# Steps of the triangular inverses moved from VectorE to GpSimd, with new durations for the planner of the order

## The chip, the cores and the metric

One core of one Trainium2 chip runs the kernel. The metric is the device time of one execution in microseconds (us): 1148.85 us before the change, the median of 3 runs. The engines are named as in the profile: PE (TensorE), DVE (VectorE), ACT (ScalarE), POOL (GpSimd), SP (SyncE, which here issues all DMAs).

## The reference

A recurrent attention over 768 time steps (4 batches x 8 heads, head size 40) is followed by two dense layers over its 3072 x 320 output.

```python
for t in range(S):                       # S = 768
    y[:, :, t] = einsum('bhd,bhde->bhe', r[t], state)
    Sa = einsum('bhde,bhe->bhd', state, a[t])
    state = state * w[t][:, :, None, :] - einsum('bhd,bhe->bhde', Sa, b[t]) + einsum('bhd,bhe->bhde', v[t], k[t])
x = y.transpose(0, 2, 1, 3).reshape(3072, 320)
h = x @ w_in;  x = (h * tanh(softplus(h))) @ w_out      # layer 1, d_ff = 2048
h = x @ w_in2; out = (h * cos(h)) @ w_out2              # layer 2
```

## The kernel before

The recurrence is computed in chunks of C = 32 time steps. The 32 (batch, head) units are split in two parts of 16, so there are 48 chunk tasks g = 0..47: chunk c = g // 2 of part g % 2. Two consecutive g, the two parts of one chunk in time, are a pair bt; there are 24 pairs.

For every g, `pre(g)` prepares the chunk: products of the decays by two scans on VectorE (`scan` L570, `rscan` L576), the scaled operands AM (`am_f`, L584) and KB (`kb_f`, L590), two memsets of AM on GpSimd (L598), the chunk's own coefficients by TensorE (`g1`, L607) and their masked copy out of PSUM by VectorE (`gev`, L617). These coefficients form, for each unit, a 32x32 triangular system, which goes to DRAM (`ldm`, L630).

For every pair, `inverse(bt)` inverts the 32 matrices of the pair. They are loaded into one half of XM as 64 rows (two 16x16 triangular blocks of each matrix), and 14 rounds, each a multiply into XT (L679) and an add into XM (L677), eliminate them by i = 1..14, over i x (15 - i) elements in each row: 14, 26, 36, 44, 50, 54, 56 and back. These 28 instructions depend each on the one before. A memset of the diagonal (L686) ends them, the result goes to DRAM and comes back as TT (L690, L694), and `halves` joins the two blocks with two matmul tasks and a transpose and a multiply on VectorE (L721, L724). XM has two halves, so two inverses can be under way.

For every g, `chain(g)` then carries the state on: `rhs` (L787), `zmm` (L801), transposes (L833), `rvz` (L859), its masked copy `rve` on VectorE (L869), `fmm` (L885), the next state and the output on VectorE (`sev` L896, `yev` L904) and transposes of the state (L929). The copies out of PSUM between them run on ScalarE (L390). Chunks are prepared up to LA = 7 ahead, as the ring of buffers for PE, AM and FL allows.

The output of two chunks in time makes a block of 256 tokens. There are 12 blocks in `layer1` (matmuls L988 and L969, with the activation on ScalarE at L1058 and L1060 and the low half GL on VectorE, L1063), then 24 tiles in `layer2` (L1003, L1019, and GL on GpSimd, L1146). The weights are split in high and low halves by `prep` (L461 to L508, the low halves on GpSimd).

No engine's order is written by hand. `Plan.run` simulates all tasks on the five engines with the durations given at `P.add`, always takes the task that can start first, with ties broken by a rank and a priority, and emits the instructions in that order. Each engine then executes its instructions in the emitted order, with semaphores for the dependences. So a duration in `P.add` changes no instruction, only where it stands. A task with `port=True` on VectorE or GpSimd is planned so that it overlaps no other such task of either engine. AGE bounds (in planned us) how long an attention task in another matmul mode is held back behind matmuls of the layers, and `lat` is the planned delay from a task to its successors.

The parts of the code that the change touches:

Of the kernel before, what the change touches and what calls it, by code (L numbers as in the profile page):

```python
# [85 lines left out]
LEAVE, CHANGE, ENTER = 0.22, 0.12, 0.13  # L86
AGE = 4.0
WAIT = 8.0
# [163 lines left out]
def body(ctx, tc, ins, out):  # L252
# [147 lines left out]
    def act(n, psum=True, ptr=0):  # L400
        return (0.05 if psum else 0.093) + 0.000833 * n + 0.093 * ptr

# [11 lines left out]
    DIRECT = 4  # L414
    HV_D, HV_P = (0.36, 0.41), 0.5
    B_HI2 = 1.0
    am_on, GLE = lambda g, d: ("DVE", 0.33), ("DVE",)
    HIE = EITHER
# [127 lines left out]
    def fifo(name, t):  # L546
        p = prev_fifo.get(name)
        if p is not None:
            t.preds.append(p)
        prev_fifo[name] = t  # L550
        return t

    def pre(g):
# [18 lines left out]

        t_sc = fifo("scan", P.add("DVE", 0.62, scan, preds=[t_ld, S_D], acq=[("PE", k("PE"))], prio=pr, port=True))
        def rscan():
# [4 lines left out]

        t_rp = P.add("DVE", 0.85, rscan, preds=[t_sc], acq=[("RP", k("RP"))], prio=pr, port=True)  # L580

# [17 lines left out]

        t_z0 = P.add("POOL", 0.24, az_f(0), preds=[t_a1], prio=pr)  # L600
        t_z1 = P.add("POOL", 0.24, az_f(1), preds=[t_z0], prio=pr)

# [19 lines left out]
        for c2 in range(2):  # L622
            for p in range(2):
                t_gl.append(P.add("DVE", 0.22, gev(p, c2), preds=[t_g], rel=[k("G")], prio=pr))
        Gev[g] = t_gl
# [27 lines left out]
    def inverse(bt):  # L653
# [15 lines left out]
        t = P.add("SP", 1.0, ld, preds=[ldma[g0 + i] for i in range(cnt)] + [S_X], acq=[("X", ("X", bt))], lat=DMA_LAT, prio=pr)  # L669

        def step(i, add):
            w = 15 - i

            def f():
                tv, b = xu()[:, :i * w].rearrange("p (j t) -> p j t", j=i), blk()
                if add:
                    V.tensor_tensor(out=b[:, 0:i, i + 1:16], in0=b[:, 0:i, i + 1:16], in1=tv, op=ALU.add)  # L677
                else:
                    V.tensor_tensor(out=tv, in0=bc(b[:, i:i + 1, i + 1:16], (2 * n, i, w)),  # L679
                                    in1=bc(b[:, 0:i, i:i + 1], (2 * n, i, w)), op=ALU.mult)  # L680
            return f

        for i in range(1, 15):
            for add in range(2):
                t = P.add("DVE", dve(i * (15 - i)), step(i, add), preds=[t], lat=0.13, prio=pr, port=True)
        t = P.add("DVE", 0.1, lambda: V.memset(x()[:, 16:512:33], 1.0), preds=[t], prio=pr)  # L686

# [81 lines left out]
    def chain(g):  # L769
# [11 lines left out]
        def rhs():  # L781
            rp = pa(k("R"))[:, 0:160].rearrange("p (g d) -> p g d", d=D)
            for n in range(NU):
# [8 lines left out]
        mated("rhs", c, t)  # L792
        t = P.add("ACT", act(160), lambda: A.activation(rs().rearrange("p g d -> p (g d)"), pa(k("R"))[:, 0:160],
                                                        AF.Copy, scale=-1.0),
# [79 lines left out]
        for h in range(2):  # L874
            ve[h] = P.add("DVE", 0.36, rve(h), preds=[r0] + z[2 * h:2 * h + 2] + [ve[i] for i in range(h)], rel=[k("V")], prio=pr)
        yb, yc = divmod(c, 2)
# [36 lines left out]
        for h, ft in ((0, f0), (1, f1)):  # L913
            s = []
            if not last:
                s = [P.add("DVE", 0.34, sev(h, p), preds=[ft, io[nx][2]], prio=pr) for p in range(2)]
            sevs += s
            rel = [k(f"F{h}")] + ([k("PE")] if h == 1 else [])
            y_acq = [("Y", ykey)] if (yc == 0 and h == 0) else []
            yevs.append(P.add("DVE", dve(128), yev(h), preds=[ft] + s + yevs, acq=y_acq, rel=rel, prio=pr + 1))  # L920
        Sev[g] = sevs
# [418 lines left out]
```

## Time and profile before

| | before |
|---|---|
| median of 3 runs | 1148.85 us (1147.74 to 1149.64) |
| the profiled execution | 1148.73 us |
| its span, first to last instruction | 1147.0 us |
| mean granted clock of TensorE | 0.952 |
| busy: PE, DVE, ACT, POOL | 1028.0, 832.9, 542.6, 228.0 us |
| inverse steps on VectorE (L679 and L677) | 336 + 336 instructions, 68.4 + 67.3 us |

The span holds three stages: attention with what is ready of layer 1 (up to about 650 us), the rest of layer 1 (to about 845 us) and layer 2. The engines' shares differ between them, so they are read by stage. A busy TensorE isn't TensorE at its peak, since its matmuls are pipelined and may run at a lower granted clock.

### The profile page before, as it was taken

Reading aid. Unit: us, or ns where it says so; the run is one execution under the profiler, and the core shown is the slowest. Engines: PE = TensorE matmul, PEld = TensorE weight load, DVE = VectorE, ACT = ScalarE, POOL = GpSimd, SP = SyncE. Lnnn points to the kernel's source line nnn. Section 1 sums busy time; section 2 is a strip of 40 time slices with the busy share of each in tenths; the row PEclk is TensorE's granted clock in tenths of the full one; section 3 lists DMA queues with packets and bytes.
Section 4 is the critical chain, followed back from the end, with each engine's and each line's share of the span. In section 5 each row is a group of like instructions: output and inputs, shape, how many; then the busy total and the mean of one; then the engine's idle time right before and its main releaser. Section 6 shows DMA issues by size and latency. Waiting matters only on the chain.

```text
span 1147.0 us, 36376 instructions
## 1 busy us (share of the span) xinstructions
PE 1028.0 (90%) x14888; PEld 941.2 (82%) x14888; DVE 832.9 (73%) x2271; ACT 542.6 (47%) x1345; POOL 228.0 (20%) x278
## 2 busy tenths in 40 slices
PE   1365888998989898998999999999999999999997
PEld 1255777888878787887888999999999999999996
DVE  8899898988888878879795378745655655555553
ACT  3345554555555465555456454444533434343433
POOL 5313111000000000000000033212333333333333
PEclk9985588999999999998999999999999999999999
DMA  8545654544545445454444345221100201010001
GB/s 248 152 128 156 163 151 107 154 114 120 147 134 148 117 118 132 116 138 138 124 113 118 112 128 162 83 81 40 44 22 1 50 2 40 12 34 4 17 7 23
DMA packets 109366, 111.88 MB, mean 98 GB/s; under 512 B 64144, under 2 KB 88720, under 8 KB 109200
## 3 DMA queue, kind: packets, MB, share of 16 engines
q1 hardware_dynamic: 109200, 109.57, 34.8%
q8 instruction: 117, 1.92, 0.7%
q14 instruction: 49, 0.40, 0.1%
HBM read 91.43 MB, written 18.09 MB: 95 GB/s over the span
## 4 chain that ended last, share of the span: by engine, by line
PE 60%; DVE 26%; issue 6%; DMA 3%; ACT 2%; SPq 1%; POOL 1%; DVEq 0%; ACTq 0%; POOLq 0%
PE bank L969 13%; PE bank L988 13%; PE bank L1003 12%; PE bank L1019 11%; DVE XT L679 3%; DVE XM L677 3%; DVE SV L896 2%; PE bank L885 2%; DVE AM L617 2%; DVE AM L584 2%; DVE RP L576 2%; DVE KB L590 2%; DVE PE L570 2%; PE bank L607 2%; DVE GL L1063 2%
## 5 line engine op out<-in xcount | busy, mean ns | idle before, releaser
L1146 POOL TENSOR_TENSOR GL<-H,GH 128x512 fp32r<-128x512 f32 x96 | 124.0, 1300 | 234.2 <-ACT GH L1144 210.7
L1130 DVE TENSOR_SCALAR T<-bank 128x512 f32<-128x512 f32 x96 | 66.1, 689 | 125.1 <-PE bank L1003 111.2
L390 ACT ACTIVATE FL<-bank 64x160 f32<-64x160 f32 (+1 forms) x375 | 101.4, 295 | 113.7 <-PE bank L640 51.6
L1137 ACT ACTIVATE T<-T,half_pi 128x512 f32<-128x512 f32 x96 | 69.4, 723 | 126.3 <-DVE T L1134 126.2
L1063 DVE TENSOR_TENSOR GL<-H,GH 128x512 fp32r<-128x512 f32 x96 | 75.5, 786 | 62.2 <-ACT GH L1060 61.0
L1058 ACT ACTIVATE H<-bank 128x512 f32<-128x512 f32 x96 | 57.4, 598 | 124.9 <-PE bank L988 124.3
L598 POOL MEMSET AM<- 64x256 f32 x96 | 29.6, 308 | 377.1 <-issue 309.2
L988 PE MATMUL bank<-XH,wih 128*128 128x256 f32 x448 | 94.3, 293 | 0.0
L988 PE MATMUL bank<-XH,wil 128*128 128x256 f32 x448 | 90.1, 283 | 0.0
L988 PE MATMUL bank<-XL,wih 128*128 128x256 f32 x448 | 90.0, 283 | 0.0
L1144 ACT ACTIVATE GH<-H 128x512 fp32r<-128x512 f32 x96 | 60.6, 631 | 51.2 <-DVE H L1139 50.1
L607 PE MATMUL bank<-AM,KB 104*64 104x64 f32 x768 | 38.3, 251 | 49.6 <-DVE KB L590 44.3
L1139 DVE TENSOR_TENSOR H<-bank,T 128x512 f32<-128x512 f32 x96 | 65.8, 685 | 19.4 <-ACT T L1137 19.3
L679 DVE TENSOR_TENSOR XT<-XM 64x14 f32<-64x14 f32 (+6 forms) x336 | 68.4, 204 | 12.5 <-DMA XM<-l_d 5.8
L607 PEld LDWEIGHTS bank<-AM,KB 104*64 104x64 f32 x768 | 31.8, 159 | 53.9 <-issue 52.4
L677 DVE TENSOR_TENSOR XM<-XM,XT 64x14 f32<-64x14 f32 (+6 forms) x336 | 67.3, 200 | 7.1
L988 PEld LDWEIGHTS bank<-XH,wih 128*128 128x128 f32 x448 | 70.2, 192 | 1.7
L885 PE MATMUL bank<-FR,FL 104*64 104x72 f32 x1536 | 64.7, 245 | 7.4 <-DVE FR L869 2.3
L988 PEld LDWEIGHTS bank<-XL,wih 128*128 128x128 f32 x448 | 69.8, 192 | 0.0
L988 PEld LDWEIGHTS bank<-XH,wil 128*128 128x128 f32 x448 | 69.8, 193 | 0.0
L885 PEld LDWEIGHTS bank<-FR,FL 104*64 104x64 f32 x1536 | 58.5, 152 | 13.6 <-DVE FR L869 3.6
L969 PE MATMUL bank<-woh1a,GL 128*128 128x320 f32 x192 | 62.7, 327 | 6.0 <-DVE GL L1063 6.0
(168 smaller groups left out, 2968.4 us busy)
## 6 DMA issues: line engine op xcount, KB each, us to landing
VR<-in_vR_dram SPq DMA_DIRECT2D x96, 160.0 KB
IN<-in_inT_dram SPq DMA_DIRECT2D x94, 161.4 KB
FR<-in_rI_dram SPq DMA_DIRECT2D x48, 180.0 KB
FR<-in_vF_dram SPq DMA_DIRECT2D x48, 144.0 KB
TMP<-in_w_in_dram SPq DMA_DIRECT2D x12, 512.0 KB
RA<-in_w_in_dram SPq DMA_DIRECT2D x12, 512.0 KB
RA<-in_w_out_dram SPq DMA_DIRECT2D x10, 512.0 KB
SV<-in_vS_dram SPq DMA_DIRECT2D x96, 52.0 KB
```

The source lines that it names most:

```text
L390: A.activation(o, i, AF.Copy)
L607: PE.matmul(gp[c0:c0 + 64, q // 2], kb()[:, q].rearrange("p a t -> p (a t)"), am()[0:104, :, q], start=True, stop=True)
L677: V.tensor_tensor(out=b[:, 0:i, i + 1:16], in0=b[:, 0:i, i + 1:16], in1=tv, op=ALU.add)
L679: V.tensor_tensor(out=tv, in0=bc(b[:, i:i + 1, i + 1:16], (2 * n, i, w)), in1=bc(b[:, 0:i, i:i + 1], (2 * n, i, w)), op=ALU.mult)
L885: PE.matmul(fp[64 * p:64 * p + 64, qp], fl()[0:104, n * D:n * D + 64], fr()[:, n], start=True, stop=True)
L969: PE.matmul(o, l[:, f, tsl], r, start=(first and f == 0 and i == 0), stop=(last and f == 1 and i == 2))
L988: PE.matmul(hp[:, f], pss[i][0], pss[i][1], start=(i == 0), stop=(i == 7))
L1003: PE.matmul(bank[P.at((key, "h"))][:, 0:512], pss[i][0], pss[i][1], start=(i == 0), stop=(i == 7))
L1019: PE.matmul(o, l, r, start=(ft == 0 and i == 0), stop=(ft == NFF - 1 and i == 2))
L1063: gl = P.add(GLE, (dve(512),), lambda eng, Hv=Hv, key=key: EN[eng].tensor_tensor(out=GL_t[P.at((key, "gl"))], in0=Hv(), in1=GH_t[P.at((key ...
L1137: c = P.add("ACT", act(512, False, 1), lambda f=f, Tv=Tv: A.activation(Tv(f), Tv(f), AF.Sin, scale=-TWO_PI, bias=half_pi), preds=[b], aset ...
L1146: gl = P.add("POOL", pool(512), lambda f=f, Hv=Hv, key=key: G.tensor_tensor(out=GL_t[P.at((key, "gl"))], in0=Hv(f), in1=GH_t[P.at((key, "g ...
```

## The change

The steps and the memset of the inverses of pairs 3 to 23 are issued on GpSimd; those of pairs 0 to 2 stay on VectorE. The planner's durations of VectorE's and ScalarE's tasks are set anew, and AGE goes from 4 to 3.

```diff
-AGE = 4.0
+AGE = 3.0
     def act(n, psum=True, ptr=0):
-        return (0.05 if psum else 0.093) + 0.000833 * n + 0.093 * ptr
+        return (0.08 if psum else 0.123) + 0.000833 * n + 0.093 * ptr
-    HV_D, HV_P = (0.36, 0.41), 0.5
+    HV_D, HV_P = (0.4, 0.43), 0.52
-    am_on, GLE = lambda g, d: ("DVE", 0.33), ("DVE",)
+    am_on, GLE = lambda g, d: ("DVE", 0.385), ("DVE",)
...
-        t_sc = fifo("scan", P.add("DVE", 0.62, scan, ...
+        t_sc = fifo("scan", P.add("DVE", 0.64, scan, ...
-        t_rp = P.add("DVE", 0.85, rscan, ...
+        t_rp = P.add("DVE", 0.91, rscan, ...
-        t_z0 = P.add("POOL", 0.24, az_f(0), ...        (t_z1 likewise)
+        t_z0 = P.add("POOL", 0.31, az_f(0), ...
-                t_gl.append(P.add("DVE", 0.22, gev(p, c2), ...
+                t_gl.append(P.add("DVE", 0.27, gev(p, c2), ...
...
+        own = bt >= 3
+        IE = G if own else V
         def step(i, add):
             w = 15 - i
             def f():
                 tv, b = xu()[:, :i * w].rearrange("p (j t) -> p j t", j=i), blk()
                 if add:
-                    V.tensor_tensor(out=b[:, 0:i, i + 1:16], in0=b[:, 0:i, i + 1:16], in1=tv, op=ALU.add)
+                    IE.tensor_tensor(out=b[:, 0:i, i + 1:16], in0=b[:, 0:i, i + 1:16], in1=tv, op=ALU.add)
                 else:
-                    V.tensor_tensor(out=tv, in0=bc(b[:, i:i + 1, i + 1:16], (2 * n, i, w)),
+                    IE.tensor_tensor(out=tv, in0=bc(b[:, i:i + 1, i + 1:16], (2 * n, i, w)),
                                     in1=bc(b[:, 0:i, i:i + 1], (2 * n, i, w)), op=ALU.mult)
             return f
         for i in range(1, 15):
             for add in range(2):
-                t = P.add("DVE", dve(i * (15 - i)), step(i, add), preds=[t], lat=0.13, prio=pr, port=True)
-        t = P.add("DVE", 0.1, lambda: V.memset(x()[:, 16:512:33], 1.0), preds=[t], prio=pr)
+                t = P.add("POOL" if own else "DVE", 0.1 + 0.0022 * i * (15 - i) if own else 0.165, step(i, add), preds=[t], lat=0.1 if own else 0.04, prio=pr, port=True)
+        t = P.add("POOL" if own else "DVE", 0.1, lambda: IE.memset(x()[:, 16:512:33], 1.0), preds=[t], prio=pr)
...
-        t = P.add("ACT", act(160), lambda: A.activation(rs()...
+        t = P.add("ACT", 0.29, lambda: A.activation(rs()...
-            ve[h] = P.add("DVE", 0.36, rve(h), ...
+            ve[h] = P.add("DVE", 0.41, rve(h), ...
-                s = [P.add("DVE", 0.34, sev(h, p), ...
+                s = [P.add("DVE", 0.315, sev(h, p), ...
-            yevs.append(P.add("DVE", dve(128), yev(h), ...
+            yevs.append(P.add("DVE", 0.26, yev(h), ...
```

## Rows read from the trace of the kernel before

**Rows 1.** Stages: length, busy of PE, PEld, DVE, ACT, POOL (instructions), granted clock, DMA
```profile
96.00:200.00 104.00, 87.25 (x1771) 77.39 (x1772) 93.28 (x297) 56.61 (x168) 19.57 (x31) 0.74 0.52 139
200.00:600.00 400.00, 369.18 (x8015) 331.05 (x8014) 339.23 (x1170) 213.41 (x642) 19.00 (x62) 0.96 0.49 130
...
600.00:650.00 50.00, 49.77 (x1130) 45.29 (x1129) 26.86 (x91) 30.05 (x85) 0.00 (x0) 1.00 0.34 96
...
600.00:1100.00 500.00, 498.28 (x4102) 468.86 (x4101) 292.86 (x519) 219.52 (x418) 140.57 (x106) 1.00 0.19 55
```

**Rows 2.** The chain that ended last from 96 to 625 us, shares by line
```profile
by line: PE bank L969 11.1%; PE bank L988 9.6%; issue 7.6%; DVE XT L679 4.8%; DVE XM L677 4.7%; DVE SV L896 4.4%; PE bank L885 3.6%; PE bank L607 3.2%; DMA TT<-t_d 3.1%; DVE AM L617 3.0%; DVE AM L584 3.0%; DVE RP L576 2.8%; DVE KB L590 2.7%
```

**Rows 3.** TensorE's waits, 200 to 600 us: total us, times, longest
```profile
PE bank L969 <- DVE GL L1063: 5.7, 6, 1.9
```

**Rows 4.** VectorE's waits, 200 to 600 us, in the same columns
```profile
DVE FR L869 <- PE bank L859: 9.0, 10, 1.6
DVE AM L617 <- PE bank L607: 7.4, 6, 2.4
DVE GL L1063 <- ACT GH L1060: 7.0, 3, 4.6
```

**Rows 5.** First step and memset of the fourth inverse (time order), then all memsets L686
```profile
96.44 1.38 DVE L679 TENSOR_TENSOR XT<-XM 64x14 f32<-64x14 f32 x2
...
125.22 0.07 DVE L686 MEMSET XM<- 64x16 f32 x1
...
L686 DVE MEMSET XM<- x24: 72/72/72, 43.6 to 623.3; 64x16 f32 x24
```

**Rows 6.** Groups on VectorE, 200 to 600 us: count, busy us, mean ns, idle before
```profile
L677 DVE TENSOR_TENSOR XM<-XM,XT 64x50 f32<-64x50 f32 (+6 forms) x229 | 44.1, 193 | 4.8
...
L617 DVE TENSOR_TENSOR AM<-bank,maskG 64x128 f32<-64x128 f32 x130 | 37.3, 287 | 12.5 <-PE bank L607 7.4 <-ACT ZS L390 2.7
L1063 DVE TENSOR_TENSOR GL<-H,GH 128x512 fp32r<-128x512 f32 x45 | 30.7, 683 | 7.5 <-ACT GH L1060 7.0
L590 DVE TENSOR_TENSOR KB<-IN,RP 104x256 f32<-104x256 f32 x66 | 27.5, 418 | 0.9
L584 DVE TENSOR_TENSOR AM<-IN,PE 40x256 f32<-40x256 f32 x65 | 27.1, 418 | 1.1
...
L576 DVE TENSOR_TENSOR_SCAN RP<-IN,D1R 104x264 f32<-104x264 f32 x32 | 22.7, 708 | 1.1
L570 DVE TENSOR_TENSOR_SCAN PE<-IN,D 104x264 f32<-104x264 f32 x32 | 22.4, 699 | 0.5
```

**Rows 7.** VectorE in time order: start us, duration, instruction
```profile
301.59 0.21 DVE L679 TENSOR_TENSOR XT<-XM 64x54 f32<-64x54 f32 x1
301.72 0.68 DVE L1063 TENSOR_TENSOR GL<-H,GH 128x512 fp32r<-128x512 f32 x1
...
305.26 0.20 DVE L679 TENSOR_TENSOR XT<-XM 64x50 f32<-64x50 f32 x1
305.50 0.20 DVE L677 TENSOR_TENSOR XM<-XM,XT 64x50 f32<-64x50 f32 x1
```

**Rows 8.** Lines L508, L1146 and L598 on GpSimd: ns min/median/max, first and last start
```profile
L508 POOL TENSOR_TENSOR wol1b<-RL,woh1b x10: 724/736/1993, 127.8 to 180.7; 128x256 fp32r<-128x256 f32 x10
...
L1146 POOL TENSOR_TENSOR GL<-H,GH x96: 1290/1301/1308, 793.1 to 1136.3; 128x512 fp32r<-128x512 f32 x96
...
L598 POOL MEMSET AM<- x96: 303/307/474, 7.6 to 576.9; 64x256 f32 x96
```

**Rows 9.** GpSimd in time order during the setup: start us, duration, instruction
```profile
3.19 0.12 POOL L379 MEMSET maskG<- 32x32 f32 x1
3.37 0.20 POOL L380 TENSOR_SCALAR_AFFINE_SELECT maskG<-maskG 32x32 f32<-32x32 f32 x1
```

**Rows 10.** Both engines in time order around 85 us
```profile
84.68 2.74 POOL L508 TENSOR_TENSOR wol1a<-H,woh1a 128x512 fp32r<-128x512 f32 x2 [19.25 <-ACT woh1a L390]
84.98 1.28 DVE L679 TENSOR_TENSOR XT<-XM 64x56 f32<-64x56 f32 x1
```

More of the change, by code (lines that the diff above doesn't have):

```diff
@@ L571, in scan @@
                                  data1=D1.rearrange("p q t -> p (q t)"), initial=0.0, op0=ALU.mult, op1=ALU.add)
-        t_sc = fifo("scan", P.add("DVE", 0.62, scan, preds=[t_ld, S_D], acq=[("PE", k("PE"))], prio=pr, port=True))
+        t_sc = fifo("scan", P.add("DVE", 0.64, scan, preds=[t_ld, S_D], acq=[("PE", k("PE"))], prio=pr, port=True))
         def rscan():
@@ L578, in rscan @@
                                  op0=ALU.mult, op1=ALU.add)
-        t_rp = P.add("DVE", 0.85, rscan, preds=[t_sc], acq=[("RP", k("RP"))], prio=pr, port=True)
+        t_rp = P.add("DVE", 0.91, rscan, preds=[t_sc], acq=[("RP", k("RP"))], prio=pr, port=True)
         def am_f(p):
@@ L598, in az_f @@
             return lambda: G.memset(am()[r, p], 0.0)
-        t_z0 = P.add("POOL", 0.24, az_f(0), preds=[t_a1], prio=pr)
-        t_z1 = P.add("POOL", 0.24, az_f(1), preds=[t_z0], prio=pr)
+        t_z0 = P.add("POOL", 0.31, az_f(0), preds=[t_a1], prio=pr)
+        t_z1 = P.add("POOL", 0.31, az_f(1), preds=[t_z0], prio=pr)
         def g1():
@@ L623, in pre @@
             for p in range(2):
-                t_gl.append(P.add("DVE", 0.22, gev(p, c2), preds=[t_g], rel=[k("G")], prio=pr))
+                t_gl.append(P.add("DVE", 0.27, gev(p, c2), preds=[t_g], rel=[k("G")], prio=pr))
         Gev[g] = t_gl
@@ L792, in chain @@
         mated("rhs", c, t)
-        t = P.add("ACT", act(160), lambda: A.activation(rs().rearrange("p g d -> p (g d)"), pa(k("R"))[:, 0:160],
+        t = P.add("ACT", 0.29, lambda: A.activation(rs().rearrange("p g d -> p (g d)"), pa(k("R"))[:, 0:160],
                                                         AF.Copy, scale=-1.0),
@@ L874, in chain @@
         for h in range(2):
-            ve[h] = P.add("DVE", 0.36, rve(h), preds=[r0] + z[2 * h:2 * h + 2] + [ve[i] for i in range(h)], rel=[k("V")], prio=pr)
+            ve[h] = P.add("DVE", 0.41, rve(h), preds=[r0] + z[2 * h:2 * h + 2] + [ve[i] for i in range(h)], rel=[k("V")], prio=pr)
         yb, yc = divmod(c, 2)
@@ L915, in chain @@
             if not last:
-                s = [P.add("DVE", 0.34, sev(h, p), preds=[ft, io[nx][2]], prio=pr) for p in range(2)]
+                s = [P.add("DVE", 0.315, sev(h, p), preds=[ft, io[nx][2]], prio=pr) for p in range(2)]
             sevs += s
@@ L919, in chain @@
             y_acq = [("Y", ykey)] if (yc == 0 and h == 0) else []
-            yevs.append(P.add("DVE", dve(128), yev(h), preds=[ft] + s + yevs, acq=y_acq, rel=rel, prio=pr + 1))
+            yevs.append(P.add("DVE", 0.26, yev(h), preds=[ft] + s + yevs, acq=y_acq, rel=rel, prio=pr + 1))
         Sev[g] = sevs
```

## Prediction

> **What bounds the kernel now.** I read the table of stages first [rows 1], because the engines' shares of the whole span mix stages with different limits. From 600 us to 1100 us TensorE is busy for 498.28 of 500 us at the full granted clock: what lies there is a fixed amount of matmul work, and nothing that VectorE is spared can shorten it. So the end is set by how much TensorE has lost before 600 us. Between 200 and 600 us (16 pairs of chunks, at the period worked out below) it is idle for 400 - 369.2 = 30.8 us, and the granted clock of 0.96 costs another 0.04 x 369 = 14.8 us: 45.6 us, or 11.4% of the stage. Between 96 and 200 us it is worse: 16.8 us idle and 0.26 x 87.25 = 22.7 us of clock (0.74 is a mean over stretches at 2.4 and at 1.2 GHz), 39.4 of 104 us, or 38%. In these stages VectorE is busy for 85% and 90% of the time. The slice from 600 to 650 us is the control: attention still runs, VectorE has fallen to 54%, and TensorE loses only 0.2 us.
>
> Next the chain of waits between 96 and 625 us [rows 2]. The two lines of the inverse's steps, L679 and L677, hold 4.8% and 4.7% of it: 9.5% of 529 us, 50 us. That is a ceiling for what their removal can give directly, as each would let the next piece of the chain come due. Last the waits: TensorE's longest is for VectorE [rows 3]; VectorE's own longest, some 7 to 9 us each in 400 us, are for TensorE and ScalarE [rows 4]. VectorE is nearly always at work, and TensorE stops for it.
>
> **The change, part 1: steps off VectorE.** The first step of the fourth inverse falls near 96.4 us; the last instruction of that inverse is at 125.22 and that of the last at 623.3 [rows 5]. The period of a pair is (623.3 - 125.2)/20 = 24.9 us. Each of 21 inverses loses 28 steps and a memset on VectorE: 588 steps of 0.193 us mean [rows 6], 113 us of busy time. Busy time isn't what the queue gives back, since neighbours overlap. A step followed by independent work takes 0.13 us until the next start (301.59 to 301.72), one followed by its dependent takes 0.24 (305.26 to 305.50) [rows 7]. Both patterns are common, so I take the middle, 0.185: 28 x 0.185 = 5.2 us a pair, bounds 3.6 and 6.7.
>
> **Part 2: steps on GpSimd.** The trace of before has no two-input operation as small as these (14 to 56 elements, mean 40). The nearest are 128x256 at 0.736 us median and 128x512 at 1.301 [rows 8]: 0.565 us for 256 elements, 2.2 ns an element, which extrapolates to 0.17 + 0.09 = 0.26 us at 40. For the hand-over between dependent instructions I take 0.06 us, the gap between a 0.12 us memset started at 3.19 and the select that starts at 3.37 [rows 9]. A step then costs 0.32 us from start to start and an inverse 28 x 0.32 = 9.0 us. The lower bound is the select's own 0.20 us (5.6 us an inverse). The upper one is the whole 0.736 + 0.06 = 0.80 us, were all of it fixed cost (22.4 us). With four memsets of AM at 0.307 us a pair [rows 8] GpSimd is busy 10 us of a pair, at worst 23.6 of 24.9. I take 0.32, the extrapolation, because the two rows are the same operation. The inverse's latency then falls or stays: now 125.2 - 96.4 = 29 us for the fourth, because its steps queue among other work.
>
> The Trainium skill speaks against this move: GPSIMD Engine Reference, section "Engine selection", keeps elementwise work on VectorE, as GpSimd is about 2x slower on two inputs. At 128x512 the trace agrees, 1.301 us on GpSimd beside 0.683 on VectorE [rows 6, 8]. By that ratio a step would be an estimated 0.39 us and an inverse 11 us, which leaves the sum below as it is, since GpSimd has the room.
>
> **Part 3: what the two engines take from each other.** While the first of two 128x512 operations ran on GpSimd from 84.68 us, a VectorE step of two SBUF inputs that started at 84.98 took 1.28 us [rows 10] instead of 0.2. So a VectorE operation with two SBUF inputs can be held for the rest of a GpSimd step. There are (66 + 65 + 32 + 32 + 45)/16 = 15 of these a pair besides the steps [rows 6]. GpSimd's steps fill 7.3 of some 20 us, 36%, and half of one is 0.13 us: 15 x 0.36 x 0.13 = 0.7 us a pair, at most 15 x 0.26 = 3.9. Net VectorE gains 5.2 - 0.7 = 4.5 us a pair, with bounds 3.6 - 3.9 = -0.3 and 6.7.
>
> The Trainium skill states the same as a lock: SBUF — State Buffer, section "Who interferes with whom", has the two engines share a port pair that one holds for a whole instruction. The rows show one case of it; the 0.7 us above is what such a lock would cost here, and the slow rival below is the case in which it costs most.
>
> **Part 4: queues.** On GpSimd the steps stand in order with the memsets of AM (L598) and, up to about 181 us, with the low halves of the first layer's weights (L508). Behind a first step that waits for its load of XM stand the memsets of later chunks, and behind them the matmuls of L607. On VectorE that same wait held everything; here it holds little, as AM has seven buffers. In the other direction a memset that waits for VectorE's AM now holds steps. I cost both at nothing, because chunks are prepared up to seven ahead, some 87 us; if that cover were gone, an inverse later by x would delay its pair by x. SyncE's stores of XM follow GpSimd's memset in place of VectorE's, which is no longer path.
>
> **Part 5: the order.** The new durations lie nearer to rows 6: L617 0.22 to 0.27 (row 0.287), L584 and L590 0.33 to 0.385 (0.418), while the planner had costed a step at 0.065 + 0.00104 x 40 = 0.107 us against 0.193. The order thus was planned for a VectorE that is faster than it is: 28 x 0.086 + 8 x 0.067 + 8 x 0.088 = 3.6 us a pair too little, on these lines alone. A truer plan should have fewer stops of TensorE for VectorE; AGE 4 to 3 lets attention cut in sooner among the FFN matmuls. No row prices a new order, it may be worth some us either way, and I cost it at nothing but keep it in the range.
>
> **The sum.** The period falls from 24.9 to 20.4 us, over 21 pairs 94 us off the attention stage. The FFN work that filled TensorE there moves behind it at full speed, so only the loss that goes with the stage is won. First end: the loss keeps its share. Steady, 17 pairs: 2.84 us a pair falls to 0.114 x 20.4 = 2.33, 8.7 us. From 96 to 200 us: 39.4 x 4.5/24.9 = 7.1 us. Together 15.8. Second end: the share falls with VectorE's load. It would be (0.848 x 24.9 - 5.4)/20.4 = 77% busy; on the line between 85% (loss 11.4%) and 54% (none) the share is 8.5%, 1.73 us a pair, and 17 x 1.11 = 18.9 us are won; likewise from 96 to 200 us at 83%, 30% of 20.4 = 6.2 in place of 9.4 us a pair, 4.2 x 3.2 = 13.4. Together 32. I take the middle, 24 us. Nothing shown decides between the two. The profiled execution took 1148.73 us around its span of 1147.0, against a median of 1148.85: 1148.7 - 24 = 1125 us. Its own range is 1106 to 1140.
>
> **The rivals.**
> TensorE keeps nothing of its loss: with VectorE free and the order truer, the steady stage becomes like that from 600 to 650 us. 17 x 2.84 = 48 us, and 7 from the first stage: 1094 us. For it: the slice from 600 us [rows 1] and the wait of rows 3. Against it: VectorE would still be 77% busy.
> VectorE wasn't the pace: the stage is paced by hand-overs between TensorE, ScalarE and the DRAM round trip of the inverse. The steady gain is nothing and half of the first stage's remains, 3.5 us: 1145 us. For it: VectorE's waits on TensorE and ScalarE [rows 4]. Against it: 50 us of steps on the chain [rows 2].
> Slower: GpSimd becomes the pace. It decides from a step spacing of 24.9/28 = 0.89 us, for which a high fixed cost (0.80) must meet waits behind VectorE's two-input operations, each up to 0.71 us [rows 6]. At 1.0 us a pair takes 28 + 1.2 = 29.2 us; 17 x 4.3 x 0.114 + 4.2 x 4.3 x 0.38 = 15 us are lost: 1164 us. Against it: the extrapolated 0.32.
>
> **How the numbers follow.** Forecast 0.58, all of the loss 0.14, VectorE not the pace 0.13, GpSimd the pace 0.15. The range 1092 to 1155 leaves out about a third of the fast case and most of the slow one. This kernel's measurements tell some 0.2%, 2.3 us, from no change. Faster by more: 0.58 + 0.14 and a third of the 0.13 less a little for a poor order, 0.75; within: 0.08; slower: 0.17.
>
> **What would show it.** L679 and L677 as GpSimd rows, 294 each, spacing near 0.32 us; VectorE below 80% from 200 us to the end of attention; memsets L686 ending near 530 us in place of 623; loss of TensorE from 96 us on down by about 24 us; stretches of at most 0.3 us on L570 to L590. Wrong: a spacing above 0.8 us, the last inverse still near 620 us, or an earlier end of attention with as much idle and slow clock as before.

## The result and the profile after

The changed kernel takes 1093.49 us, the median of 4 runs (1089.86 to 1094.91), beside 1149.24 us (1147.74 to 1149.80) of the kernel before, run in turn with it: ratio 0.9512, 95% interval 0.9486 to 0.9538, a gain of 55.7 us. The profiled execution took 1094.35 us around a span of 1092.6. The time lies in the range, at the rival in which TensorE keeps nothing of its loss (1094), and not at the forecast of 1125: the gain is more than twice the 24 us of the sum.

The accounting comes first. Both kernels issue 14,888 matmuls. The page's row of engines for after (busy us, share of the span, instructions):

```profile
PE 1008.8 (92%) x14888; PEld 926.3 (85%) x14888; DVE 743.6 (68%) x1661; ACT 545.2 (50%) x1346; POOL 437.3 (40%) x887
```

Before, TensorE was busy for 1028.0 us of the span of 1147.0, so idle for 119.0. Now it is 1008.8 of 1092.6, idle for 83.8. Of the 54.4 us that the span lost, 35.2 are idle time and 19.2 are the same matmuls in less busy time.

The stages of after, which answer to [rows 1]: length, busy us of PE, PEld, DVE, ACT and POOL with their instructions, granted clock of TensorE, DMA share, GB/s. The line on top is before's first stage, which [rows 1] doesn't have; the others are after's.

```profile
0.00:96.00 96.00, 34.01 (x784) 28.39 (x784) 86.28 (x255) 36.55 (x93) 33.42 (x68) 0.90 0.62 179
```

```profile
0.00:96.00 96.00, 38.87 (x894) 32.62 (x896) 88.39 (x255) 37.92 (x99) 30.36 (x68) 1.00 0.64 180
96.00:200.00 104.00, 96.84 (x2048) 86.57 (x2046) 87.80 (x225) 67.38 (x194) 58.66 (x147) 0.93 0.56 151
200.00:600.00 400.00, 390.79 (x8865) 354.70 (x8866) 274.10 (x729) 233.72 (x698) 189.86 (x555) 1.00 0.54 143
...
600.00:650.00 50.00, 48.14 (x364) 46.93 (x363) 45.90 (x66) 24.36 (x44) 17.69 (x11) 1.00 0.48 146
```

From 200 to 600 us TensorE's idle time fell from 30.8 to 9.2 us and the granted clock rose from 0.96 to 1.00, that is, to 2.4 GHz throughout; from 96 to 200 us the idle time fell from 16.8 to 7.2 and the clock rose from 0.74 to 0.93. In the last row attention is over: the last matmul of L888 starts at 592.6 us, where before it (L885) was 652.5. VectorE's 92% there is GL and the weights of layer 2, and TensorE runs 364 long FFN matmuls and loses 1.9 us of 50. So the row can't be set beside the slice from 600 to 650 us in [rows 1], and says nothing for or against the sum.

The steps are GpSimd's now: engine and operation, count, ns min/median/max, first and last start.

```profile
L682 POOL TENSOR_TENSOR XT<-XM x294: 205/280/1575, 95.0 to 561.1; 64x14 f32<-64x14 f32 x21, 64x36 f32<-64x36 f32 x21, 64x50 f32<-64x50 f32 x21, 64x56 f32<-64x56 f32 x21
L680 POOL TENSOR_TENSOR XM<-XM,XT x294: 205/281/1795, 95.2 to 561.4; 64x14 f32<-64x14 f32 x21, 64x36 f32<-64x36 f32 x21, 64x50 f32<-64x50 f32 x21, 64x56 f32<-64x56 f32 x21
...
L689 POOL MEMSET XM<- x21: 115/122/127, 106.3 to 561.6; 64x16 f32 x21
```

The multiplies stand at L682 and the adds at L680 (L679 and L677 before; lines behind them are three further down). The last inverse ends at 561.6 us, where it was 623.3 [rows 5]: the period is (561.6 - 106.3)/20 = 22.8 us, not the 20.4 of the sum.

TensorE's longest waits from 200 to 600 us, then VectorE's (total us, times, longest):

```profile
PE bank L804 <- issue: 2.9, 4, 1.1
PE bank L719 <- DVE TA L724: 1.9, 1, 1.9
PE bank L836 <- DVE AM L617: 1.1, 1, 1.1
```

```profile
DVE GL L1066 <- ACT GH L1063: 32.0, 10, 9.8
DVE AM L617 <- PE bank L607: 19.0, 11, 5.2
DVE TA L724 <- DMA TT<-t_d: 14.8, 7, 3.4
```

The wait of [rows 3] is gone from the head of the list, and what is left is small. VectorE now waits for ScalarE and TensorE instead, 32.0 and 19.0 us where [rows 4] had 7.0 and 7.4. The chain of waits from 96 to 562 us by line, which answers to [rows 2], has no step of an inverse among the lines that the row shows:

```profile
by line: PE bank L991 16.3%; PE bank L972 16.2%; PE bank L888 6.9%; issue 4.5%; PE bank L862 3.9%; PE bank L607 3.4%; PE bank L932 3.1%; PE bank L640 3.0%; PE bank L836 2.8%; PE bank L790 2.7%; PE bank L719 2.7%; DVE SV L899 2.5%; PE bank L
```

### The profile page after: what moved, and what is told of

Same layout as the page of the kernel before. It is cut to its first block, busy times and chain, and to the rows that moved or that the text cites. A ratio compares the mean times of both kernels' runs of the same rounds, so it can differ in the third digit from the quotient of the medians.

```text
span 1092.6 us, 36346 instructions
## 1 busy us (share of the span) xinstructions
PE 1008.8 (92%) x14888; PEld 926.3 (85%) x14888; DVE 743.6 (68%) x1661; ACT 545.2 (50%) x1346; POOL 437.3 (40%) x887
## 4 chain that ended last, share of the span: by engine, by line
PE 62%; DVE 12%; issue 11%; POOL 6%; DMA 5%; ACT 4%; SPq 1%; POOLq 0%; DVEq 0%; ACTq 0%
PE bank L991 15%; PE bank L972 15%; PE bank L1006 8%; PE bank L1022 7%; POOL GL L1149 4%; PE bank L888 4%; PE bank L862 2%; PE bank L607 1%; PE bank L932 1%; PE bank L836 1%; PE bank L640 1%; DVE SV L899 1%; PE bank L790 1%; PE bank L804 1%; PE bank L719 1%
## 5 line engine op out<-in xcount | busy, mean ns | idle before, releaser
L682 POOL TENSOR_TENSOR XT<-XM 64x14 f32<-64x14 f32 (+6 forms) x294 | 102.2, 348 | 176.2 <-DMA XM<-l_d 155.3
L1066 DVE TENSOR_TENSOR GL<-H,GH 128x512 fp32r<-128x512 f32 x96 | 70.7, 740 | 70.8 <-ACT GH L1063 70.2
L680 POOL TENSOR_TENSOR XM<-XM,XT 64x14 f32<-64x14 f32 (+6 forms) x294 | 106.1, 361 | 22.5
L607 PE MATMUL bank<-AM,KB 104*64 104x64 f32 x768 | 36.9, 246 | 48.1 <-DVE KB L590 39.6
L617 DVE TENSOR_TENSOR AM<-bank,maskG 64x128 f32<-64x128 f32 x192 | 55.1, 287 | 31.4 <-PE bank L607 20.2
L607 PEld LDWEIGHTS bank<-AM,KB 104*64 104x64 f32 x768 | 30.5, 155 | 52.5 <-issue 38.6
L991 PE MATMUL bank<-XH,wix 128*128 128x256 f32 x224 | 67.4, 301 | 0.9 <-issue 0.9
L1137 DVE SCALAR_TENSOR_TENSOR T<-T,bank 128x512 f32<-128x512 f32 x96 | 65.7, 684 | 2.2
L888 PE MATMUL bank<-FR,FL 104*64 104x72 f32 x1536 | 63.7, 240 | 3.6 <-ACT wih L390 2.0
```

The costliest lines, as they stand in the source:

```text
L607: PE.matmul(gp[c0:c0 + 64, q // 2], kb()[:, q].rearrange("p a t -> p (a t)"), am()[0:104, :, q], start=True, stop=True)
L680: IE.tensor_tensor(out=b[:, 0:i, i + 1:16], in0=b[:, 0:i, i + 1:16], in1=tv, op=ALU.add)
L682: IE.tensor_tensor(out=tv, in0=bc(b[:, i:i + 1, i + 1:16], (2 * n, i, w)), in1=bc(b[:, 0:i, i:i + 1], (2 * n, i, w)), op=ALU.mult)
L888: PE.matmul(fp[64 * p:64 * p + 64, qp], fl()[0:104, n * D:n * D + 64], fr()[:, n], start=True, stop=True)
L991: PE.matmul(hp[:, f], pss[i][0], pss[i][1], start=(i == 0), stop=(i == 7))
L1066: gl = P.add(GLE, (dve(512),), lambda eng, Hv=Hv, key=key: EN[eng].tensor_tensor(out=GL_t[P.at((key, "gl"))], in0=Hv(), in1=GH_t[P.at((key ...
```

## The experiments

Three theories were to be told apart. A: TensorE's loss goes with VectorE's busy share (the sum). B: the steps cost what they do because they are a chain of 28 dependent instructions, with an end that is due, in the in-order queue that also serves TensorE; their busy time matters little. C: the truer plan of part 5 brings the gain, and the engine of the steps is secondary.

All runs in one table. The ratio is to runs of before in turn with them. "Idle" is the span of the profiled execution less TensorE's busy time; the last column is the start of the memset that ends the last inverse.

| kernel | median us | ratio to before, 95% | TensorE busy, idle | last inverse ends |
|---|---|---|---|---|
| before | 1149.24 | | 1028.0, 119.0 | 623.3 |
| after | 1093.49 | 0.9486 to 0.9538 | 1008.8, 83.8 | 561.6 |
| e1 steps moved, old durations | 1093.25 | 0.9441 to 0.9535 | 1003.2, 86.7 | 586.1 |
| e2 new durations, steps on VectorE | 1167.55 | 1.0091 to 1.0196 | 1034.2, 131.7 | 629.8 |
| e4 after, other tie-break | 1099.36 | 0.9505 to 0.9586 | 1013.9, 83.2 | 575.9 |
| e5 before, other tie-break | 1138.69 | 0.9857 to 0.9927 | 1023.3, 115.3 | 616.1 |
| e16 before, dearer step in the plan | 1148.80 | 0.9972 to 1.0033 | 1020.3, 124.8 | 611.4 |
| e17 e2, other tie-break | 1146.81 | 0.9946 to 1.0009 | 1025.3, 119.2 | 614.0 |
| e3 load on VectorE, not in the plan | 1163.92 | 1.0069 to 1.0131 | 1046.9, 113.7 | 626.3 |
| e7 half that load, not in the plan | 1126.76 | 0.9704 to 0.9837 | 1023.3, 101.4 | 592.4 |
| e11 load on VectorE, planned | 1112.91 | 0.9618 to 0.9714 | 1014.3, 96.1 | 621.4 |
| e14 the load as a chain, planned | 1118.61 | 0.9703 to 0.9732 | 1017.0, 100.5 | 593.9 |
| e15 the chain, with its end due | 1137.49 | 0.9858 to 0.9902 | 1025.8, 110.5 | 615.6 |
| e9 multiplies twice on GpSimd, not in the plan | 1157.64 | 1.0023 to 1.0082 | 1035.3, 120.7 | 629.5 |
| e10 the same, planned | 1099.24 | 0.9495 to 0.9597 | 1011.8, 84.9 | 609.6 |
| e12 every second inverse moved | 1106.35 | 0.9558 to 0.9674 | 1010.2, 92.6 | 590.1 |
| e13 no steps at all from pair 3 on | 1101.61 | 0.9515 to 0.9617 | 1005.1, 94.2 | 539.3 |
| e8 all inverses moved | 1105.56 | 0.9539 to 0.9635 | 1017.8, 88.6 | 568.6 |

### The move alone, and the durations alone

e1 is the kernel before with the steps and the memset of pairs 3 to 23 on GpSimd, and nothing else of the change:

```diff
+        own = bt >= 3
+        IE = G if own else V
...
-                t = P.add("DVE", dve(i * (15 - i)), step(i, add), preds=[t], lat=0.13, prio=pr, port=True)
-        t = P.add("DVE", 0.1, lambda: V.memset(x()[:, 16:512:33], 1.0), preds=[t], prio=pr)
+                t = P.add("POOL" if own else "DVE", 0.1 + 0.0022 * i * (15 - i) if own else dve(i * (15 - i)), step(i, add), preds=[t], lat=0.1 if own else 0.13, prio=pr, port=True)
+        t = P.add("POOL" if own else "DVE", 0.1, lambda: IE.memset(x()[:, 16:512:33], 1.0), preds=[t], prio=pr)
```

> The kernel before with only the steps and the memset of pairs 3 to 23 on GpSimd (planned there at 0.1 + 0.0022 n us, 0.1 us to the next); every other duration and AGE as before. If the 55 us come from VectorE's freed time (load theory), this run has most of them: 1095 to 1112 us, and TensorE's idle time from 200 to 600 us falls from 31 us to below 15. If they come from an order planned with true durations (order theory), it stays at 1130 to 1150 us, with TensorE still stopped for VectorE.

e2 is the kernel after with the steps back on VectorE:

```diff
-        own = bt >= 3
+        own = False
```

> The changed kernel with all inverse steps on VectorE (planned at 0.165 us), so only the new durations and AGE 3 against the kernel before. Load theory: VectorE stays near 85% busy from 200 to 600 us and the time is 1135 to 1155 us. Order theory: 1095 to 1115 us with the same VectorE load.

e1 gives 1093.25 us, all that the change gives; e2 gives 1167.55, 18 us more than before. The stage from 200 to 600 us of e1, with e2's below it:

```profile
200.00:600.00 400.00, 388.41 (x8562) 352.48 (x8561) 270.29 (x711) 225.21 (x673) 168.95 (x539) 0.99 0.51 136
```

```profile
200.00:600.00 400.00, 360.85 (x8023) 322.63 (x8025) 334.97 (x1133) 208.33 (x631) 18.95 (x62) 0.92 0.49 128
```

and e2's longest waits of TensorE in that stage:

```profile
PE bank L607 <- DVE KB L590: 14.4, 4, 6.9
PE bank L607 <- DVE XM L680: 6.9, 1, 6.9
```

In e2 TensorE idles for 39.2 us in place of 30.8, with 14.4 us of it behind one product of VectorE's queue and 6.9 behind a step itself. Theory C falls: the truer plan is worth nothing where the steps stay, and where they go the old plan does as well. As e1 also keeps AGE at 4, that part of the change brings nothing that can be seen beside e1; it was not tried by itself.

### How much a newly drawn order is worth

Any edit of a duration redraws the planned order. e4 and e5 change only the constant TIE, from which the planner scatters its durations by up to 1%, so that ties break otherwise, in after and in before; e17 does so in e2; e16 is before with the step alone given its truer cost.

```diff
-TIE = 97
+TIE = 11
```

```diff
-                t = P.add("DVE", dve(i * (15 - i)), step(i, add), preds=[t], lat=0.13, prio=pr, port=True)
+                t = P.add("DVE", 0.165, step(i, add), preds=[t], lat=0.04, prio=pr, port=True)
```

> The changed kernel with another constant (TIE 11 for 97) in the 1% scatter that the planner puts on its durations: another order of the same quality. It measures what one drawing of the order is worth. Load and order theory alike: 1088 to 1105 us. If 97 was a lucky drawing, it is 1110 to 1130 us.

> The kernel before with TIE 11 for 97: another drawing of its order, all steps on VectorE. If the order matters little while VectorE is the pace, 1140 to 1165 us; if the drawing alone can carry the gain, below 1120 us.

> The kernel before with one planner entry changed: a step costs 0.165 us and 0.04 to the next, in place of 0.065 + 0.00104 n and 0.13. All steps stay on VectorE. If the too small cost of a step made the kernel before slow (TensorE's order was planned for a faster VectorE), 1110 to 1135 us; if a truer cost doesn't help as long as the steps are there, 1140 to 1170 us.

> e2_durations_only with TIE 11 for 97, another drawing of its order. If e2's 1168 us are the steps on VectorE, 1140 to 1175 us; if they were an unlucky drawing, 1105 to 1135 us.

With the steps on VectorE, five orders take 1138.69, 1146.81, 1148.80, 1149.24 and 1167.55 us; with the steps moved, three take 1093.25, 1093.49 and 1099.36. The two groups don't touch: 39 us lie between the best of the one and the worst of the other. Within a group the tie-break alone moved the time by up to 21 us (e2 to e17), and the five orders of the first group, which also differ in durations, span 29. That is the yardstick for what follows: a difference of under some 20 us between two orders, or of under 29 where durations differ too, is not by itself a cause.

### The load put back on VectorE

If A holds, work of the same length on VectorE must bring the time back, whoever waits for it. e3 leaves after's order as planned and issues behind every step on GpSimd a multiply on VectorE into a scratch tile XD that nobody reads (64x24, 588 in all; XM and TMP are a little smaller to make room). e7 does so at the multiplies alone, 294.

```diff
...
+                if own:
+                    V.tensor_tensor(out=XD[0:64], in0=ident[0:64, 0:24], in1=ident[0:64, 64:88], op=ALU.mult)
```

> The changed kernel in its own planned order, with one more VectorE multiply of 64x24 elements on a scratch tile beside each step that runs on GpSimd: 588 instructions of some 0.18 us, which depend on nothing and which the planner doesn't know. VectorE's load is back, the move and the order stay. Load theory: most of the gain goes, 1125 to 1150 us, and TensorE's clock and idle time from 200 to 600 us are those of before (0.96, 31 us). If neither VectorE's load but the latency of the inverse or the order made the gain, it stays below 1105 us.

> As e3_load_back, but the added VectorE multiply stands beside every second step only (the multiplies): 294 instructions of 0.186 us, half of the load. If TensorE's loss falls in proportion to VectorE's load, as the straight line of the prediction has it, the time is in the middle between 1093 and 1164: 1120 to 1135 us. If the loss appears only once VectorE has no time left (a kink), it is 1093 to 1110 us.

e3 came out at 1163.92 and e7 at 1126.76 us, the middle between after and e3. By itself that looked like A. But here the planner didn't know of the load, and with it every later instruction of VectorE's fixed order came later than planned. e11 issues the same 588 multiplies as tasks of their own, for which the planner finds the place, behind a step and with nothing that depends on them:

```diff
...
+        def load():
+            V.tensor_tensor(out=XD[0:64], in0=ident[0:64, 0:24], in1=ident[0:64, 64:88], op=ALU.mult)
...
+                if own:
+                    P.add("DVE", 0.165, load, preds=[t], prio=pr, port=True)
```

> e3_load_back with the planner told: each added VectorE multiply is a task of 0.165 us, released with the step beside which it stood. If VectorE's load itself takes the gain, the time is 1130 to 1165 us as in e3 and with the steps on VectorE. If e3 was slow only because VectorE ran behind its planned order, it returns to 1095 to 1115 us.

The stage from 200 to 600 us of e3, then that of e11:

```profile
200.00:600.00 400.00, 371.13 (x7895) 333.76 (x7887) 326.23 (x1143) 211.19 (x635) 180.84 (x535) 0.93 0.50 130
```

```profile
200.00:600.00 400.00, 392.13 (x8382) 354.43 (x8383) 344.15 (x1171) 226.63 (x664) 178.36 (x553) 0.99 0.50 131
```

The load's own group on VectorE in that stage, of e3 and then of e11 (count, busy us, mean ns, idle before), is of the same size in both:

```profile
L686 DVE TENSOR_TENSOR XD<-ident 64x24 f32<-64x24 f32 x443 | 82.6, 186 | 8.0
```

```profile
L688 DVE TENSOR_TENSOR XD<-ident 64x24 f32<-64x24 f32 x460 | 84.7, 184 | 12.1
```

e11 takes 1112.91 us. VectorE is busy for 344.15 us of 400 in it, more than the 339.23 of before, in 1171 instructions beside 1170; and its last inverse ends at 621.4, beside 623.3 of before. Yet TensorE idles for 7.9 us where before had 30.8, at a clock of 0.99. For this stage A falls: nothing of what it goes by has changed against before, and most of TensorE's loss is gone. A redrawn order doesn't explain it, since in this stage TensorE idles for 22.1 to 39.1 us in the five orders with the steps on VectorE and for 9.2 to 11.6 in the three with the steps moved. The whole time is 36 us less than before's.

Between 96 us, where the moved inverses begin, and 200 us it is otherwise. e11 there:

```profile
96.00:200.00 104.00, 82.98 (x1700) 73.43 (x1696) 93.48 (x285) 58.13 (x167) 47.11 (x120) 0.86 0.53 141
```

Here VectorE is busy for 93.48 us, as in before (93.28), and TensorE idles for 21.0 us, among the 16.1 to 29.5 of the five orders and not the 5.3 to 7.2 of the three. So for this stage e11 doesn't refute A, and most of what e11 takes longer than after is lost here. The load that was free to be placed costs 19 us, no more than a redrawn order may; the 51 us between e3 and e11 are the price of the same work where the order doesn't know of it.

### From free load to chain

e14 makes the load a chain, each multiply behind the one before, as the steps were; e15 has the memset that ends the inverse wait for that chain, on VectorE, so that the chain's end is due as the steps' end was.

```diff
+        d = None
...
-                    P.add("DVE", 0.165, load, preds=[t], prio=pr, port=True)
+                    d = P.add("DVE", 0.165, load, preds=[d or t], lat=0.04, prio=pr, port=True)
```

```diff
-        t = P.add("POOL" if own else "DVE", 0.1, lambda: IE.memset(x()[:, 16:512:33], 1.0), preds=[t], prio=pr)
+        t = P.add("DVE", 0.1, lambda: V.memset(x()[:, 16:512:33], 1.0), preds=[t, d], prio=pr)
```

> As e11_load_planned, but the added VectorE multiplies of one inverse are planned as a chain, each after the one before, 0.04 us apart, as the steps are on VectorE; nothing waits for them. If the form of a chain in VectorE's queue is the cause, 1140 to 1165 us; if it isn't, 1105 to 1120 us as in e11.

> As e14_chain_load, and the memset that ends the inverse stands on VectorE behind the last of the chain, so that the inverse's result waits for the chain as it does with the steps on VectorE. If a chain with a due time in VectorE's queue is the cause, 1140 to 1165 us while e14 stays near 1113; if neither, 1105 to 1122 us.

The difference between e11 and e14 lies in the plan alone. All multiplies write the one tile XD, and where two stand next to each other in VectorE's order they start 0.21 us apart (median) in both runs; e11's plan put 421 of 588 directly before another, e14's 155.

1112.91 us as a free load, 1118.61 as a chain, 1137.49 as a chain that is waited for; the steps themselves on VectorE took 1139 to 1168. TensorE's idle time is 7.9, 18.1 and 17.9 us of the stage from 200 to 600 us, and 21.0, 16.3 and 23.7 of that from 96 to 200. The waits of TensorE in e15 from 200 to 600 us have the chain in them:

```profile
PE bank L726 <- DVE XD L688: 3.1, 1, 3.1
...
PE bank L608 <- DVE XD L688: 2.5, 2, 1.8
```

The row of values is what B expects, and 44 us lie between its ends, after and e15. But its single steps, 6 and 19 us, are within the yardstick, each rests on one order, and in e15 an inverse waits for two chains, its own on GpSimd and the load on VectorE, which can make it longer than the steps on VectorE alone did. So B agrees with the runs and is not settled by them.

### GpSimd's own time

e9 issues every multiply on GpSimd twice, the second one unknown to the planner; e10 is the same code with its cost told.

```diff
+                    if own:
+                        G.tensor_tensor(out=tv, in0=bc(b[:, i:i + 1, i + 1:16], (2 * n, i, w)),
+                                        in1=bc(b[:, 0:i, i:i + 1], (2 * n, i, w)), op=ALU.mult)
```

```diff
-                t = P.add("POOL" if own else "DVE", 0.1 + 0.0022 * i * (15 - i) if own else 0.165, step(i, add), preds=[t], lat=0.1 if own else 0.04, prio=pr, port=True)
+                t = P.add("POOL" if own else "DVE", (1 if add else 2.3) * (0.16 + 0.0022 * i * (15 - i)) if own else 0.165, step(i, add), preds=[t], lat=0.1 if own else 0.04, prio=pr, port=True)
```

> The changed kernel with each multiply that runs on GpSimd issued twice, the second unplanned: 294 more GpSimd steps, some 14 x 0.36 = 5 us more for each inverse, VectorE untouched. The slow rival (GpSimd the pace) expects 1110 us or more. If GpSimd's 155 us of waiting for XM are slack, the time stays at 1090 to 1102 us.

> e9_multiplies_twice with the planner told: the doubled multiply is planned at 2.3 x (0.16 + 0.0022 n) us, the add at 0.16 + 0.0022 n. If GpSimd as such became the pace in e9 (some 15 us a pair of its own steps), the time stays near 1150 us. If e9 was slow because GpSimd ran behind the order that was planned for it, so that memsets and loads stood in the wrong places, the time returns to 1090 to 1110 us.

The stage from 200 to 600 us of e9, and TensorE's longest wait in it:

```profile
200.00:600.00 400.00, 363.43 (x7740) 328.47 (x7736) 258.60 (x687) 208.53 (x628) 246.99 (x741) 0.92 0.50 129
```

```profile
PE bank L607 <- POOL AM L598: 16.9, 6, 5.7
```

The same stage of e10:

```profile
200.00:600.00 400.00, 395.03 (x8387) 359.76 (x8385) 274.09 (x714) 231.67 (x678) 262.57 (x790) 1.00 0.50 132
```

e10 takes 1099.24 us with 14 more steps an inverse, at 0.36 us each 5 us: GpSimd's time is hidden. It also answers a rival, that the move pays because the inverse itself becomes shorter. From its first step to its memset an inverse of pairs 4 to 23 takes 18.1 us on average in before, 13.7 in after and 19.6 in e10, which is longer than in before and keeps the gain. e9, the same work, takes 1157.64 and loses the whole gain. TensorE idles for 36.6 us of the stage in e9 and for 5.0 in e10, and the row of waits names 16.9 us of the difference: the memset of AM for a later chunk stands in GpSimd's order behind steps that come later than planned, and the matmuls of L607 behind the memset, for up to 5.7 us.

### No steps, every second inverse, all inverses

e13 leaves the 28 steps of pairs 3 to 23 out on every engine, and with them the inverses of these pairs. e12 moves every second inverse from the fourth pair on, e8 moves those of the first three pairs as well.

```diff
-        for i in range(1, 15):
+        for i in range(1, 15 if bt < 3 else 1):
```

```diff
-        own = bt >= 3
+        own = bt >= 3 and bt % 2 == 1
```

```diff
-        own = bt >= 3
+        own = True
```

> The kernel before without the 28 steps of the inverses of pairs 3 to 23 on any engine (that part of the computation is left out; load, memset and store stay). The bound of what the move can give: VectorE is relieved and GpSimd costs nothing. If GpSimd's slower steps, their waits for VectorE and their place in its queue are hidden, it is within 8 us of the move alone (1085 to 1095 us); if they cost, 1065 to 1080 us.

> The changed kernel with the steps of pairs 3, 5, ..., 23 on GpSimd and those of pairs 4, 6, ..., 22 on VectorE: 11 of 21 inverses moved, all of it planned. Straight line between none (1167 us, e2) and all (1093 us): 1125 to 1135 us. Kink (no loss as long as VectorE has some time left): 1095 to 1112 us.

> The changed kernel with the steps of all 24 pairs on GpSimd. VectorE is 92% busy in the first 96 us, TensorE idle for 57 of them. Load theory: relief there shortens the start too, 1080 to 1092 us. Against it: in the start the inverse lies on the path of the first chunks, and with some 0.35 us a step beside 0.24 on VectorE and the weights' low halves in the same queue each inverse comes later: 1094 to 1110 us.

e13 takes 1101.61 us: without any steps the kernel, in before's remaining plan, is not faster than with the steps on GpSimd, so nothing that they still cost there can be seen in this one order. e12 takes 1106.35, with 305.75 us of VectorE's time from 200 to 600:

```profile
200.00:600.00 400.00, 389.23 (x8683) 353.54 (x8684) 305.75 (x951) 232.03 (x692) 99.23 (x323) 1.00 0.52 136
```

With 11 of 21 inverses moved it gives 43 of the 56 us, where a gain in proportion would be 29, for 1120; that is 14 us off proportion, within the yardstick. e8 takes 1105.56 us, 12 more than after; the profiled spans are 13.8 apart, 4.8 of idle time and 9.0 of busy time. Its granted clock is lower in the two first stages, 0.89 and 0.78 where after has 1.00 and 0.93:

```profile
0.00:96.00 96.00, 44.32 (x1160) 37.86 (x1162) 74.37 (x176) 38.93 (x106) 53.75 (x151) 0.89 0.63 178
96.00:200.00 104.00, 88.86 (x1699) 78.43 (x1698) 78.64 (x203) 61.83 (x177) 56.28 (x137) 0.78 0.54 146
```

The memset that ends the first inverse starts at 50.9 us in e8 and at 44.7 in after, so the first inverse is slower on GpSimd. Whether that costs the 12 us or the redrawn order does isn't told apart. No run was faster than after and e1.

## Why the prediction was right or wrong

**What bounds the kernel.** Right: the loss of TensorE before 600 us was what could be won, and the work behind attention had next to nothing to give. The sentence that TensorE stops because VectorE is nearly always at work was not, for the steady stage from 200 to 600 us: there e11 has VectorE as much at work, and TensorE idles for 7.9 us in place of 30.8. The 50 us that the steps hold of the chain of waits were called a ceiling for what the removal gives directly; the move alone (e1) gave 56.

**Part 1, VectorE's time.** Right in what leaves the queue: VectorE's busy time a pair went from 339.23/16.06 = 21.1 to 274.10/17.54 = 15.6 us, 5.5 us, and 5.2 net of overlap had been taken. Its busy share is 68.5%, below the 77% forecast.

**Part 2, the steps on GpSimd.** The extrapolation held for a step alone: it lasts 0.21 us (64x14) to 0.29 (64x56), and the next of the long ones starts 0.36 behind (313.88, 314.24, 314.60 below); 0.26 and 0.32 had been taken, the bounds were 0.20 and 0.80. A whole inverse was taken at 9.0 us and needs 13.7 on average, inside its bounds of 5.6 and 22.4, in part since VectorE holds some of the steps (last section). GpSimd in time order:

```profile
313.52 0.28 POOL L680 TENSOR_TENSOR XM<-XM,XT 64x50 f32<-64x50 f32 x1
313.88 0.28 POOL L682 TENSOR_TENSOR XT<-XM 64x54 f32<-64x54 f32 x1
314.24 0.28 POOL L680 TENSOR_TENSOR XM<-XM,XT 64x54 f32<-64x54 f32 x1
314.60 0.28 POOL L682 TENSOR_TENSOR XT<-XM 64x56 f32<-64x56 f32 x1
```

**Part 3, the lock.** The size was off and the direction too. VectorE's operations with two SBUF inputs, the groups of [rows 6], from 200 to 600 us in after (count, busy us, mean ns):

```profile
L584 DVE TENSOR_TENSOR AM<-IN,PE 40x256 f32<-40x256 f32 x62 | 26.4, 425 | 0.8
L590 DVE TENSOR_TENSOR KB<-IN,RP 104x256 f32<-104x256 f32 x62 | 25.0, 420 | 2.0 <-PE bank L640 1.9
L576 DVE TENSOR_TENSOR_SCAN RP<-IN,D1R 104x264 f32<-104x264 f32 x31 | 22.1, 714 | 1.1
L570 DVE TENSOR_TENSOR_SCAN PE<-IN,D 104x264 f32<-104x264 f32 x31 | 22.0, 708 | 0.3
```

They are longer by 2 to 9 ns (418, 418, 708, 699 before). With L1066 (683 to 689) that is 62 x 7 + 62 x 2 + 31 x 6 + 31 x 9 + 52 x 6 = 1.3 us over 17.5 pairs, 0.08 us a pair where 0.7 had been taken. The time is paid on GpSimd's side, as the section on the hardware shows.

**Part 4, queues at nothing.** Right for the change as it stands, since the planner knows what a step costs on GpSimd and TensorE has no notable wait on L598. It was right by little: where each inverse is 5 us longer than planned, this term has the largest of the waits that cost 58 us (e9 beside e10). The cover that was named, chunks prepared up to seven ahead, did not hold there.

**Part 5, the order at nothing.** Right: e1 without the new durations has the time of after. The reasoning that a truer plan stops TensorE less was wrong, by e2, e16 and e17, none of them faster than before by more than 0.6%.

**The sum.** Here the prediction failed, in two links. The first: the period falls by what VectorE is spared, from 24.9 to 20.4 us. It fell to 22.8, and to 23.9 in e1 ((586.1 - 107.7)/20), which has the same time. In e10 it is 24.9 ((609.6 - 112.3)/20), before's period, and the gain of 50 us is there all the same. So the gain doesn't go by the period; that a full TensorE leaves to the order how much FFN work stands between two pairs would explain it, and no run tries that by itself. The second: TensorE's loss follows VectorE's load, in share or on a line, to 8.5 or 11.4% of the steady stage. It fell to 9.2 us of 400, 2.3%, at a clock of 1.00. Even at the measured 68.5% the line would have left 11.4 x (68.5 - 54)/(85 - 54) = 5.3%; e11 at 86% has 7.9 us of idle time and 0.01 x 392 = 3.9 of clock, 2.9%, where the line gives above 11.4. From 96 to 200 us the rule is not refuted: there e11 loses 21.0 us and 0.14 x 82.98 = 11.6 of clock, 31% of the stage, beside the 38% that the prediction read in before. The middle between two ends of one wrong rule was no bound at all.

One term in both ends was mis-sized the other way. The clock was priced as (1 - granted clock) x busy time. By that price 0.10 x 34.01 = 3.4, 22.7 and 14.8 us were lost to it in the three stages before, 40.9 us, and 0.07 x 96.84 = 6.8 in after, a fall of 34 us (the last 40 to 50 us of each run, granted 0.95 and 0.94, cost 2 us in both). The same matmuls became shorter by 19.2 us in all. Nor does the busy time follow the clock elsewhere: before and e5 have mean granted clocks of 0.952 and 0.983, 0.031 x 1028 = 32 us by that price, and busy times that are 4.7 us apart. So here the product overstates what the clock gives back. That the rival's 1094 meets the measured time is thus partly luck: it counted 48 us from 200 us on and 7 before it, and measured are 35.2 us of idle time (4.9 before 96 us, 9.6 from 96 to 200, 21.6 from 200 to 600, 0.9 given back behind) and 19.2 of busy time. The sum and the rival had no term for the time before 96 us; the 4.9 us there come with the new durations, since e2, which moves nothing, has after's 57.1 us of idle time in that stage.

**The rivals.** "TensorE keeps nothing" had the outcome; the reason against it, that VectorE would still be 77% busy, was no reason. "VectorE wasn't the pace" was right that the period need not follow VectorE's time (e10) and wrong to conclude that nothing is won; what does set the period is not shown. "GpSimd becomes the pace" is refuted: 0.36 us from step to step, where it decides from 0.89, and e10 adds half the steps again without harm. The slow side was real by another mechanism, a delay that the fixed order doesn't know of (e9, 1158).

**What stays open.** Shown: the gain comes from the steps leaving VectorE (e1 beside e2, five orders beside three), and from 200 to 600 us it is not VectorE's busy share that makes it (e11), nor is it a shorter inverse alone (e10). Not settled: whether the busy share matters from 96 to 200 us, and how much of the 56 us is due to the chain, how much to its due end, and how much to what a fixed order can't foresee, since the steps from e11 to e15 are as small as the difference between two orders.

## What to carry to other kernels

Judge work in an in-order queue by what stands behind it and when its own end is due, not by the engine's busy share: from 200 to 600 us an engine at 86% starved nobody here once its work could be placed freely. Where an order is fixed by a planner, whatever is added to a queue must be told to the planner at its real length; the same work cost 51 and 58 us more where it was not. Before a planned order's change is called a cause, redraw the order once by its tie-break: here that alone moved the time by 6 to 21 us.

## What the runs showed of the hardware

VectorE and GpSimd don't hold each other alike where GpSimd's instructions are short. Both engines of after in time order (start us, duration):

```profile
300.95 0.28 POOL L680 TENSOR_TENSOR XM<-XM,XT 64x50 f32<-64x50 f32 x1
...
301.21 0.69 DVE L570 TENSOR_TENSOR_SCAN PE<-IN,D 104x264 f32<-104x264 f32 x1
301.31 0.68 POOL L682 TENSOR_TENSOR XT<-XM 64x54 f32<-64x54 f32 x1
...
302.18 0.74 DVE L576 TENSOR_TENSOR_SCAN RP<-IN,D1R 104x264 f32<-104x264 f32 x1
302.43 0.57 POOL L682 TENSOR_TENSOR XT<-XM 64x56 f32<-64x56 f32 x1
302.84 0.44 DVE L584 TENSOR_TENSOR AM<-IN,PE 40x256 f32<-40x256 f32 x1
303.08 0.70 POOL L680 TENSOR_TENSOR XM<-XM,XT 64x56 f32<-64x56 f32 x1
303.21 0.41 DVE L590 TENSOR_TENSOR KB<-IN,RP 104x256 f32<-104x256 f32 x1
```

A step of 0.28 us takes 0.57 to 0.70 where it begins inside a VectorE operation with two SBUF inputs, and ends about 0.1 us behind that operation: 301.21 + 0.69 = 301.90, and the step ends at 301.99. The last one begins inside L584 and ends at 303.78, behind L590, which had followed. From 200 to 560 us 115 steps began inside such an operation (L570, L576, L584, L590, L1066) and lasted 0.59 us on average, 320 began and ran clear of them and lasted 0.26. In the other direction, 129 of these operations of VectorE began inside a step, and were longer than the 103 others of their lines by 0.016 us on average. While VectorE reads one input from PSUM (L899 and L907 around 313 to 315 us) the steps keep to 0.28. The starts on GpSimd are the profiler's and rough, but the lengths on VectorE are not.

The Trainium skill, SBUF — State Buffer, section "Who interferes with whom", has the shared port pair as an exclusive lock, and issue order decide which of the two is blocked. The trace agrees for GpSimd's steps (0.28 to 0.68) and for a VectorE step behind a long GpSimd operation (1.28 us, [rows 10]); for VectorE behind the short steps it shows 0.016 us. The Trainium skill, Perfetto Trace Analysis, section "Optimizing Scalar/DVE Operations", says of the two engines' common read port that moving work between them might not help; here it gave 55.7 us.
